# Moving two operations of a weight conversion from GpSimd to VectorE in a fused attention and MLP kernel

## The chip, the cores and the metric

The kernel runs on one core of a Trainium2 chip. The metric is the device time of one execution in microseconds (us). The core has TensorE (PE, matrix products; PEld is its weight load), VectorE (DVE), ScalarE (ACT), GpSimd (POOL), and queues that issue DMAs, here mostly that of SyncE (SP). The engines run side by side and meet at semaphores. Each engine works through its own instructions in a fixed order.

## The reference

Three layers, one behind the other, in float32. Shapes: batch 8, 8 heads, sequence 576, head width 64, 128 features; model width 512, inner width 1024.

```
# attention by features
proj = x @ w_phi;  proj -= max(|proj|) over features
phi(x) = concat(exp(proj), exp(-proj))
out = phi(q) @ (phi(k)^T v) / (phi(q) @ sum(phi(k)) + 1e-6)
# first MLP
xk = mu_k * x + (1 - mu_k) * x_prev     # x_prev: x shifted by one step
xr = mu_r * x + (1 - mu_r) * x_prev
k = relu(xk @ w_k);  v = (k * k) @ w_v;  r = sigmoid(xr @ w_r);  x = r * v
# second MLP
h = relu(x @ w_in);  c = conv over 3 steps of h;  out = (h * sigmoid(c)) @ w_out
```

The weights arrive as float64.

## The kernel before, in words

**Attention** works on 32 pairs of heads (`Pi`, four pairs to a batch). `block(Pi)` writes the work around one pair: at its head the transposes of pair Pi's centred q (`turn`, `turn_end`; tiles `pt`, `pr`), then the projection of k of pair Pi+2 (`front`; tiles `p`, `pk`, centred by VectorE as `mx` and `t`), of q of pair Pi+1 (`pq`), the sums over k and v (`sums4`, tile `pkv`), the quotients (`results`; tiles `pn`, `rd`, `xn`) and ScalarE's exponentials (`features`, tile `kp`). `column(Pi - 1)` and `column_end` transpose the finished pair's `xn` into `xT` (tile `px`). For pairs 1 to 3 that stands behind `front`; from `MS` = 4 on it stands at the head of the block, ahead of `turn`, so pair 3's transpose opens block 4.

**First MLP.** `moe(u)` works on half a batch u: mixed inputs (`xf`, `mh`, `ml`), eight products with w_k (`psk`), ReLU into `kf`, its square (VectorE, line 460), its high part `kh` (ScalarE) and low part `kl` (VectorE), four products with w_r (`psr`) and four with w_v (`psv`). Each float32 product is three matmuls of high and low parts (`mm3`, lines 149 to 151). From block 4 on `feed` puts 6, 6, 7, 9 and then 10 steps of it behind each block. TensorE runs in the order in which the program is written; the other engines' order is laid out by the framework's scheduler, which plans with modelled times, except where `behind` holds an instruction behind the one written before it on the same engine.

**The weights' conversion.** w_k, w_r and w_v are converted from float64 in 20 parts of 128 x 512 (`step`): a DMA into `raw` (two buffers), then a tick later ScalarE takes the absolute value of the high word into `h` (two buffers) and GpSimd clamps it, a tick later VectorE does a shift and two combining operations, a tick later ScalarE writes the high part (`wkh`, `wrh`, `wvh`) and GpSimd subtracts it to give the low part (`wkl`, ...). Each `tick` moves every part under way by one stage and starts the next part. So tick t brings the shift of part t-3 (counted from 0), and `ready` is t-3. Ticks stand twice in each of blocks 0 to 6 and, by `WAT`, nine more times behind blocks 4 to 6: 23 in all, as many as 20 parts need. `want(n)` adds ticks where a product needs parts that are not written yet. The tick that starts part i+2 waits on the SP queue for part i's `raw` buffer, which the second combining operation frees. w_in and w_out are converted later, by lines 120 to 134, in smaller parts (`hc`), still with GpSimd.

**Second MLP** runs after all that, from about 850 us, on the same engines.

Of the kernel before, what the change touches and what calls it, by code (L numbers as in the profile page):

```python
# [12 lines left out]
ALU = mybir.AluOpType  # L13
# [15 lines left out]
MS, SLOW, SR = 4, 8, {4: 6, 5: 6, 6: 7, 7: 9}  # L29

WAT = {4: (4, 10), 5: (3, 7, 11), 6: (3, 5, 7, 9)}
DS0 = 10
HS = S // 2
V1 = D + 1

# [6 lines left out]
def fused_kernel(ctx: ExitStack, tc: tile.TileContext, qk, va, wphi, ones2, mu, wk, wv, wr, win, wout, cw, out):  # L42
# [25 lines left out]
    V, A, G = Noted(nc.vector), Noted(nc.scalar), Noted(nc.gpsimd)  # L68
# [7 lines left out]
    def f(x):  # L76
        return x.bitcast(F32)
# [78 lines left out]
    with ExitStack() as p1:  # L156
# [10 lines left out]
        def step(src, hs, ls, o):  # L167
            o_ = slice(o, o + 512)
            raw = pool.tile([P, 512, 2], U32, tag="raw", bufs=2, name="raw")
            SY.dma_start(raw, src[:, o_])  # L170
            yield
            h = pool.tile([P, 512], F32, tag="h", bufs=2, name="h")
            high, low, hu = raw[:, :, 1], raw[:, :, 0], h.bitcast(U32)
            A.behind("activation", h, f(high), AF.Abs, scale=2.0 ** -16)
            G.behind("tensor_scalar", h, h, 2.0 ** -31, 122879.9921875 * 2.0 ** -16, ALU.max, ALU.min)
            yield
            V.behind("tensor_scalar", hu, hu, 3, None, ALU.logical_shift_left)
            V.scalar_tensor_tensor(hu, low, 29, hu, ALU.logical_shift_right, ALU.bitwise_or)
            V.scalar_tensor_tensor(hu, high, 0x7FFFFFFF, hu, ALU.bitwise_or, ALU.bitwise_and)
            yield  # L180
            A.behind("copy", hs[:, o_], h)
            G.behind("tensor_tensor", ls[:, o_], h, f(hs[:, o_]), ALU.subtract)
            ready[0] += 1

        under, ready = [], [0]

        def tick():
            for x in list(under):
                if next(x, 1) == 1:
                    under.remove(x)  # L190
            if wsteps:
                x = wsteps.pop(0)
                next(x)
                under.append(x)

        wsteps = [step(wk, wkh, wkl, o) for o in range(0, 4096, 512)]
        for h in range(2):
            for w in ((wr, wrh, wrl), (wv, wvh, wvl)):
                n = w[1].shape[1] // 2
# [13 lines left out]
        def load(Pi):  # L213

            b, p = divmod(Pi, NP)
            raw = pool.tile([P, W], F32, tag="x", bufs=3, name="rqk")
            if Pi == 0:
                for c in (slice(KC0, W), slice(0, KC0)):
                    SY.dma_start(raw[:, c], qk[b, p, :, c])
            else:  # L220
                (SY if Pi < 5 else G).dma_start(raw, qk[b, p])
            xk[Pi] = raw
# [86 lines left out]
        def column_end(xn, xt, px):  # L309
            T.transpose(px[:, :P], xn[:, 4], ident)  # L310

            def copies():
                for h in range(2):
                    r = slice(64 * h, 64 * h + 64)
                    A.copy(xt[r, 513:577], px[r, r])
            return copies
# [46 lines left out]
        def block(Pi):  # L363

            nq, nk = Pi + 1 < B * NP, Pi + 2 < B * NP
            if 0 <= Pi < B * NP - 3:
                load(Pi + 3)
            if Pi >= 0:
                if Pi >= MS:
                    x = column(Pi - 1)  # L370
                qf, t1 = turn(Pi)
                pr = psa.tile([P, 512], F32, tag="at", name="pr")
                if Pi >= MS:
                    copies = column_end(*x, pr)
                turn_end(qf, t1, pr)
                if Pi >= MS:
                    copies()
            if nk:
                tk = front(Pi + 2)
            if 0 <= Pi < 7:  # L380
                tick()
            if 1 <= Pi < MS:
                x = column(Pi - 1)
                column_end(*x, psm.tile([P, 512], F32, tag="mm", name="pr"))()
            if nq:
                ts[Pi + 1] += centre4(rows4(Pi + 1, 0, "pq"), "tq")
                del xk[Pi + 1]
                sums4(Pi + 1)
            if Pi >= 0:
                results(Pi, qf)  # L390
            if nk:
                features(Pi + 2, tk)
                if Pi + 2 > 1:
                    load_v(Pi + 2)
            if 0 <= Pi < 7:
                tick()

        def attention(Pi):
# [8 lines left out]
        def mix(u, j):  # L407

            b, hf = divmod(u, 2)
            o = hf * HS  # L410
            hi = main.tile([P, KC, HS], F32R, tag="mh", bufs=2, name=f"mh{j}")
            lo = main.tile([P, KC, HS], F32R, tag="ml", bufs=2, name=f"ml{j}")
            for c0 in range(0, KC, 2):
                xf = tmps.tile([P, 2, HS], F32, tag="tmp", name="xf")
                for c in range(c0, c0 + 2):
                    A.activation(xf[:, c - c0], xT[b, c][:, 1 + o:1 + o + HS], AF.Copy, scale=mu0[:, j, c:c + 1])
                    V.scalar_tensor_tensor(xf[:, c - c0], xT[b, c][:, o:o + HS], mu1[:, j, c:c + 1], xf[:, c - c0], ALU.mult, ALU.add)
                A.copy(hi[:, c0:c0 + 2], xf)
# [16 lines left out]

        def want(n):

            while ready[0] < n:
                tick()

        def moe(u):
            b, hf = divmod(u, 2)
            o = hf * HS
            for j in range(2):
                while not mix_next(u, j):
                    yield
            xh, xl = mixed.pop((u, 0))
            k2 = []
            for fp in range(FC // 2):
                kf = tmps.tile([P, 2, HS], F32, tag="tmp", name="kf")  # L450
                for j in range(2):
                    ps = psm.tile([P, 512], F32, tag="mm", name="psk")[:, :HS]
                    fc = 2 * fp + j
                    want(fc + 1)
                    for c in range(KC):
                        w = slice(fc * DM + c * P, fc * DM + c * P + P)
                        mm3(ps, wkh[:, w], wkl[:, w], xh[:, c], xl[:, c], c == 0, c == KC - 1)
                    A.activation(kf[:, j], ps, AF.Relu)
                    yield
                V.tensor_tensor(kf, kf, kf, ALU.mult)  # L460
                kh = main.tile([P, 2, HS], F32R, tag="kh", bufs=4, name="kh")
                kl = main.tile([P, 2, HS], F32R, tag="kl", bufs=4, name="kl")
                A.copy(kh, kf)
                V.tensor_tensor(kl, kf, f(kh), ALU.subtract)
                k2.append((kh, kl))
            rh, rl = mixed.pop((u, 1))
            for mp in range(2):
                sg = main.tile([P, 2, HS], F32, tag="sg", bufs=1, name="sg")
                for j in range(2):
                    ps = psm.tile([P, 512], F32, tag="mm", name="psr")[:, :HS]  # L470
                    mc = 2 * mp + j
                    want(9 + 6 * mp + j)
                    for c in range(KC):
                        w = slice(mc * DM + c * P, mc * DM + c * P + P)
                        mm3(ps, wrh[:, w], wrl[:, w], rh[:, c], rl[:, c], c == 0, c == KC - 1)
                    A.activation(sg[:, j], ps, AF.Tanh, scale=0.5)
                    yield
                mix_next(u + 1, mp)
                x2 = tmps.tile([P, 2, HS], F32, tag="tmp", name="x2")
                for j in range(2):  # L480
                    ps = psm.tile([P, 512], F32, tag="mm", name="psv")[:, :HS]
                    mc = 2 * mp + j
                    want(12 + 6 * mp + 2 * j)
                    for kc in range(FC):
                        w = slice(mc * DFF + kc * P, mc * DFF + kc * P + P)
                        kh, kl = k2[kc // 2]
                        mm3(ps, wvh[:, w], wvl[:, w], kh[:, kc % 2], kl[:, kc % 2], kc == 0, kc == FC - 1)
                    yield
                    V.scalar_tensor_tensor(x2[:, j], sg[:, j], 1.0, ps, ALU.add, ALU.mult)
                    yield  # L490
                SY.dma_start(x2s[b][:, 2 * mp:2 * mp + 2, o:o + HS], x2)
# [14 lines left out]
        def extras(Pi, n):  # L506
            if n in WAT.get(Pi, ()):
                tick()
            if Pi == 7 and n == 14:
                taps()  # L510
            if Pi >= DS0 and dsteps and n in (3, 11):
                dsteps[0] = dsteps[0][0](), dsteps[0][1]
            if Pi >= DS0 and dsteps and n in (4, 12):
                raw, step = dsteps.pop(0)
# [10 lines left out]
        with tc.manual_schedule(engines={mybir.EngineType.PE}):  # L525
# [6 lines left out]
            x = column(B * NP - 1)  # L532
# [160 lines left out]
```

## Time and profile before

| what | value |
|---|---|
| median of 3 runs | 1251.81 us (1251.13 to 1252.43) |
| the profiled execution | 1253.4 us |
| its span, first to last instruction | 1251.6 us |
| TensorE busy | 1210.5 us, 97% |
| VectorE busy | 771.0 us, 62% |
| ScalarE busy | 697.2 us, 56% |
| GpSimd busy | 133.9 us, 11% |
| mean granted clock of TensorE | 0.985 |

The profiled execution took 1253.4 us, 1.8 us more than the span that the trace covers and 1.6 us more than the median of the runs. Shares are over the whole span; the stretch that the change touches is its first eighth, and there they are others. A row of a stretch gives its start and end, its length, the busy time (and instructions) of PE, PEld, DVE, ACT and POOL, TensorE's mean granted clock as a share of 2.4 GHz, the busy share of the DMA engines and GB/s. A row of a group gives the total busy us, the mean ns of one, and the idle time ahead of them with what ended it; a row in order of time the start, the us, and in brackets the idle time before.

### The profile page before, as it was taken

The numbers are of one execution on the slowest core, as the hardware profiler recorded it, in microseconds if no ns is written. First come the engines' busy times: TensorE is split into PE (matmuls) and PEld (weight loads), VectorE is DVE, ScalarE is ACT, GpSimd is POOL, SyncE is SP. The second block draws the span as 40 slices with busy tenths as digits, with TensorE's granted clock in tenths as the row PEclk, the third lists the DMA queues.
The fourth block names the chain that finished last, engine by engine and source line by source line (L and its number), as shares of the span: only waits on it lengthen the run. The fifth ranks groups of instructions, "written<-read, shape, count | busy, mean of one in ns | idle before, by whom it ended". The sixth has DMA issues, their size and how long they took to land.

```text
span 1251.6 us, 29156 instructions
## 1 busy us (share of the span) xinstructions
PE 1210.5 (97%) x12000; PEld 1149.2 (92%) x12000; DVE 771.0 (62%) x1560; ACT 697.2 (56%) x1644; POOL 133.9 (11%) x219
## 2 busy tenths in 40 slices
PE   8798599999999999999999999999999999999998
PEld 7687599999999999999999999998888888888887
DVE  6989564767657657757655534425556655575555
ACT  6867274655656546646645534425555555565554
POOL 1445500111111111011000000000000000000000
PEclk9998699999999999999999999999999999999999
DMA  5534321223223223322220004050122011210210
GB/s 176 163 116 139 95 71 50 74 84 111 87 84 112 87 84 92 119 84 91 65 66 27 13 20 145 20 183 11 61 61 61 6 56 61 61 31 31 62 61 31
DMA packets 55956, 95.56 MB, mean 76 GB/s; under 512 B 10000, under 2 KB 38800, under 8 KB 55824
## 3 DMA queue, kind: packets, MB, share of 16 engines
q1 hardware_dynamic: 42544, 68.17, 16.9%
q0 software_dynamic: 3920, 15.93, 4.2%
q10 hardware_dynamic: 9360, 9.61, 2.8%
q8 instruction: 94, 1.54, 0.5%
q14 instruction: 38, 0.31, 0.1%
HBM read 66.42 MB, written 27.26 MB: 75 GB/s over the span
## 4 chain that ended last, share of the span: by engine, by line
PE 87%; DVE 6%; ACT 3%; issue 2%; DMA 2%; POOL 1%; SPq 0%; ACTq 0%; DVEq 0%; POOLq 0%
PE psh L149 5%; PE psh L151 5%; PE psh L150 5%; PE psv L149 5%; PE psv L150 5%; PE psv L151 5%; PE psk L150 5%; PE psk L151 5%; PE psk L149 5%; PE pkv L293 5%; PE pso L149 5%; PE pso L151 5%; PE pso L150 5%; PE pn L346 4%; PE psr L149 3%; PE psr L150 3%
## 5 line engine op out<-in xcount | busy, mean ns | idle before, releaser
L149 PE MATMUL psv<-kh,wvl 128*128 128x288 f32 x512 | 154.1, 301 | 11.6 <-POOL wvl L57 10.7
L57 DVE SCALAR_TENSOR_TENSOR ct<-h,cw,ct 128x460 f32<-128x460 f32 (+2 forms) x160 | 111.4, 697 | 85.2 <-ACT ct L57 84.1
L150 PE MATMUL psv<-kl,wvh 128*128 128x288 f32 x512 | 153.3, 300 | 2.1 <-DVE kl L57 2.1
L151 PE MATMUL psv<-kh,wvh 128*128 128x288 f32 x512 | 153.1, 299 | 0.0
L149 PE MATMUL psk<-mh,wkl 128*128 128x288 f32 x512 | 150.7, 294 | 1.3 <-ACT kf L57 1.3
L150 PE MATMUL psk<-ml,wkh 128*128 128x288 f32 x512 | 151.0, 295 | 0.0
L151 PE MATMUL psk<-mh,wkh 128*128 128x288 f32 x512 | 150.9, 295 | 0.0
L151 PE MATMUL psh<-xh,wih 128*128 128x462 f32 (+1 forms) x320 | 118.9, 372 | 0.0
L150 PE MATMUL psh<-xl,wih 128*128 128x462 f32 (+1 forms) x320 | 118.8, 372 | 0.0
L150 PE MATMUL pso<-gl,woh 128*128 128x460 f32 (+1 forms) x320 | 118.0, 371 | 0.0
L151 PE MATMUL pso<-gh,woh 128*128 128x460 f32 (+1 forms) x320 | 118.0, 371 | 0.0
L57 ACT ACTIVATE kf<-psk 128x288 f32<-128x288 f32 x128 | 52.2, 409 | 109.3 <-PE psk L151 108.5
L149 PEld LDWEIGHTS psv<-kh,wvl 128*128 128x128 f32 x512 | 97.9, 191 | 14.3 <-POOL wvl L57 12.3
L149 PE MATMUL psh<-xh,wil 128*128 128x462 f32 (+1 forms) x320 | 107.3, 372 | 0.0
L150 PEld LDWEIGHTS psv<-kl,wvh 128*128 128x128 f32 x512 | 98.2, 192 | 2.3 <-DVE kl L57 2.3
L151 PEld LDWEIGHTS psv<-kh,wvh 128*128 128x128 f32 x512 | 98.3, 192 | 0.0
L149 PEld LDWEIGHTS psk<-mh,wkl 128*128 128x128 f32 x512 | 96.3, 188 | 2.0 <-issue 1.3
L57 DVE TENSOR_TENSOR kf<-kf 128x576 f32<-128x576 f32 x64 | 48.7, 761 | 79.3 <-ACT kf L57 79.3
L150 PEld LDWEIGHTS psk<-ml,wkh 128*128 128x128 f32 x512 | 96.3, 188 | 0.0
L151 PEld LDWEIGHTS psk<-mh,wkh 128*128 128x128 f32 x512 | 96.2, 188 | 0.0
L57 DVE SCALAR_TENSOR_TENSOR x<-sg,psv 128x288 f32<-128x288 f32 x64 | 29.1, 454 | 108.1 <-PE psv L151 104.1
L57 ACT ACTIVATE h<-psh 128x462 f32<-128x462 f32 (+3 forms) x128 | 47.9, 410 | 75.5 <-PE psh L151 74.3
(96 smaller groups left out, 2866.5 us busy)
## 6 DMA issues: line engine op xcount, KB each, us to landing
rqk<-qk POOLq DMA_DIRECT2D x27, 576.0 KB, 4.7
va<-va SPq DMA_DIRECT2D x32, 325.0 KB, 4.2
x2s<-x SPq DMA_DIRECT2D x32, 288.0 KB, 2.2
raw<-wk SPq DMA_DIRECT2D x8, 512.0 KB, 3.5
raw<-wv SPq DMA_DIRECT2D x8, 512.0 KB, 3.5
raw<-win SPq DMA_DIRECT2D x16, 256.0 KB, 2.9
raw<-wout SPq DMA_DIRECT2D x16, 256.0 KB, 3.0
x2r<-x2s ACTq DMA_DIRECT2D x16, 231.0 KB, 2.7
```

Source lines behind the costliest of these rows:

```text
L57: x = op(*a, **k)
L149: T.matmul(ps, wl, xh, start=first, stop=False)
L150: T.matmul(ps, wh, xl, start=False, stop=False)
L151: T.matmul(ps, wh, xh, start=False, stop=last)
L293: T.matmul(o[r:r + 64], k_[:, r:r + 64], v_, start=(i == 0), stop=(i == len(prods) - 1))
L346: T.matmul(pn[b_][64 * r:64 * r + 64, j], qf[h_][:, c, o:o + 64], kv[:, c, h_], start=(j == 0 and c == 0), stop=(j == 4 - b_ and c == 1))
```

## The change

Five edits. VectorE takes the clamp and the low part's subtraction of the 20 parts from GpSimd; within a tick the high part's copy on ScalarE is now written first, then VectorE's operations of the next part, then the subtraction, then the absolute value, then the next load. Ticks also stand in block -1. `want` asks for two parts more than the product needs (`AHEAD`). ScalarE squares `kf` for the first batch (u = 0 and 1). Pair 3's `column` moves from the head of block 4 to the place behind `front`, with its last piece in a `psm` tile.

```diff
+AHEAD = 2
...
             A.behind("activation", h, f(high), AF.Abs, scale=2.0 ** -16)
-            G.behind("tensor_scalar", h, h, 2.0 ** -31, 122879.9921875 * 2.0 ** -16, ALU.max, ALU.min)
             yield
-            V.behind("tensor_scalar", hu, hu, 3, None, ALU.logical_shift_left)
+            V.behind("tensor_scalar", h, h, 2.0 ** -31, 122879.9921875 * 2.0 ** -16, ALU.max, ALU.min)
+            V.tensor_scalar(hu, hu, 3, None, ALU.logical_shift_left)
...
             A.behind("copy", hs[:, o_], h)
-            G.behind("tensor_tensor", ls[:, o_], h, f(hs[:, o_]), ALU.subtract)
+            yield
+            V.behind("tensor_tensor", ls[:, o_], h, f(hs[:, o_]), ALU.subtract)
             ready[0] += 1
...
-            for x in list(under):
-                if next(x, 1) == 1:
-                    under.remove(x)
+            for at in (3, 2, 4, 1):
+                for x in under:
+                    if x[1] == at:
+                        next(x[0], None)
+                        x[1] += 1
+            if under and under[0][1] == 5:
+                under.pop(0)
             if wsteps:
-                x = wsteps.pop(0)
-                next(x)
-                under.append(x)
+                under.append([wsteps.pop(0), 1])
+                next(under[-1][0])
...
-                if Pi >= MS:
+                if Pi > MS:
                     x = column(Pi - 1)
...
-            if 0 <= Pi < 7:
+            if -1 <= Pi < 7:
                 tick()
-            if 1 <= Pi < MS:
+            if 1 <= Pi <= MS:
                 x = column(Pi - 1)
...
-            while ready[0] < n:
+            while ready[0] < min(n + AHEAD, 20):
                 tick()
...
-                V.tensor_tensor(kf, kf, kf, ALU.mult)
+                if u < 2:
+                    A.square(kf, kf)
+                else:
+                    V.tensor_tensor(kf, kf, kf, ALU.mult)
```

## Rows read from the trace of the kernel before

**Rows 1.** The page's 40 slices: TensorE's granted clock in tenths.
```profile
PEclk9998699999999999999999999999999999999999
```
**Rows 2.** Stretches, blocks 0, 1, 4 to 7: length, then busy by engine.
```profile
15.20:23.80 8.60, 8.49 (x192) 7.92 (x190) 6.11 (x13) 8.01 (x23) 0.00 (x0) 1.00 0.45 137
23.80:33.80 10.00, 9.39 (x199) 8.54 (x195) 8.69 (x20) 8.37 (x24) 4.37 (x3) 1.00 0.25 82
...
62.35:85.11 22.76, 21.41 (x267) 20.48 (x268) 18.53 (x36) 15.24 (x37) 10.41 (x9) 0.87 0.41 129
85.11:112.40 27.29, 20.71 (x270) 19.15 (x269) 26.02 (x45) 19.11 (x46) 17.16 (x11) 0.94 0.37 112
112.40:155.65 43.25, 29.76 (x293) 27.36 (x292) 30.03 (x51) 18.43 (x43) 23.18 (x20) 0.74 0.38 115
155.65:177.65 22.00, 22.00 (x293) 21.64 (x293) 12.67 (x27) 12.48 (x33) 0.62 (x1) 0.97 0.18 58
```
**Rows 3.** The same view, all that follows block 6.
```profile
155.65:1251.60 1095.95, 1090.49 (x10272) 1038.88 (x10271) 643.86 (x1315) 599.30 (x1407) 62.04 (x155) 1.00 0.22 68
```
**Rows 4.** TensorE's waits, 0 to 156 us: total, times, longest.
```profile
PE psv L149 <- POOL wvl L57: 10.7, 5, 3.1
PE px L305 <- DVE xn L57: 5.2, 1, 5.2
```
**Rows 5.** The chain that ended last, 130 to 142 us.
```profile
130.18 3.60 DMA raw<-wv
...
133.87 0.69 ACT h L57
...
134.63 1.92 POOL h L57
...
136.72 1.26 issue
...
141.07 3.57 DMA raw<-wv
```
**Rows 6.** VectorE's instructions on `h`, 15.2 to 112.4 us: ns min/median/max, first and last start.
```profile
L57 DVE SCALAR_TENSOR_TENSOR h<-raw,h x26: 674/680/1664, 32.2 to 110.7; 128x512 uint32<-128x512 uint32 x26
L57 DVE TENSOR_SCALAR h<-h x13: 414/953/1500, 29.8 to 108.0; 128x512 uint32<-128x512 uint32 x13
```
**Rows 7.** VectorE's groups by form, 20 to 156 us.
```profile
L57 DVE SCALAR_TENSOR_TENSOR h<-raw,h 128x512 uint32<-128x512 uint32 x40 | 30.9, 772 | 0.5
L57 DVE TENSOR_SCALAR h<-h 128x512 uint32<-128x512 uint32 x20 | 19.2, 959 | 5.2 <-POOL h L57 5.2
...
L57 DVE TENSOR_TENSOR ml<-xf,mh 128x576 fp32r<-128x576 f32 x8 | 7.3, 914 | 0.0
...
L57 DVE TENSOR_TENSOR kf<-kf 128x576 f32<-128x576 f32 x4 | 3.2, 804 | 1.1 <-ACT kf L57 1.1
...
L57 DVE TENSOR_TENSOR kl<-kf,kh 128x576 fp32r<-128x576 f32 x4 | 3.0, 749 | 0.1
```
**Rows 8.** VectorE on `hc`, half as wide: ns min/median/max.
```profile
L57 DVE TENSOR_SCALAR hc<-hc x32: 282/286/290, 227.8 to 616.2; 128x256 uint32<-128x256 uint32 x32
L57 DVE TENSOR_TENSOR whl<-hc,whl x32: 415/418/420, 232.3 to 618.0; 128x256 fp32r<-128x256 f32 x32
```
**Rows 9.** VectorE in order of time.
```profile
62.47 0.42 DVE L57 TENSOR_SCALAR h<-h 128x512 uint32<-128x512 uint32 x1
...
66.57 0.29 DVE L57 TENSOR_REDUCE mx<-p 128x1 f32<-128x128 f32 x1 [2.24 <-PE p L236]
...
126.61 1.49 DVE L57 TENSOR_SCALAR h<-h 128x512 uint32<-128x512 uint32 x1 [0.53 <-POOL h L57]
```
**Rows 10.** GpSimd in order of time.
```profile
126.55 1.25 POOL L57 TENSOR_TENSOR wrh<-h,wrh 128x512 fp32r<-128x512 f32 x1
```
**Rows 11.** ScalarE's groups: `kh` (60 to 160 us) and table loads (whole span).
```profile
L57 ACT CAST kh<-kf 128x576 fp32r<-128x576 f32 x4 | 2.7, 682 | 2.2 <-DVE kf L57 2.2
...
L57 ACT ACT_TABLE_LOAD x2 | 2.6, 1283 | 1.2 <-PEq L684 1.2
```
**Rows 12.** ScalarE's waits, 20 to 156 us.
```profile
ACT h L57 <- DMA raw<-wv: 9.1, 4, 3.1
```

More of the change, by code (lines that the diff above doesn't have):

```diff
@@ L372, in block @@
                 pr = psa.tile([P, 512], F32, tag="at", name="pr")
-                if Pi >= MS:
+                if Pi > MS:
                     copies = column_end(*x, pr)
                 turn_end(qf, t1, pr)
-                if Pi >= MS:
+                if Pi > MS:
                     copies()
@@ L394, in block @@
                     load_v(Pi + 2)
-            if 0 <= Pi < 7:
+            if -1 <= Pi < 7:
                 tick()
```

## The prediction

> **What bounds the kernel now.** I read the 40 slices first. TensorE's granted clock is near full in all of them but the first few, and lowest in the fifth [rows 1]. Then the busy time by stretch, cut at each block's first transposes. From 155.65 us on TensorE is busy 1090.49 of 1095.95 us [rows 3]: nothing that VectorE, ScalarE or GpSimd do there is on the path, so the change can win or lose only ahead of that point. Block 6, 112.40 to 155.65 us, is where time lies open. It has 293 matmuls, as block 7 has, but takes 43.25 us where block 7 takes 22.00 with TensorE never idle; its clock is granted at 0.74, against 0.97 there [rows 2]. In block 5 VectorE is the full engine, 26.02 of 27.29 us. TensorE's waits say what is late: five times a low part that GpSimd wrote (10.7 us), and once, at the head of block 4, pair 3's `xn` (5.2 us) [rows 4]. The chain shows how block 6 goes round: a load (3.60 us), the absolute value, GpSimd's clamp (1.92), a gap of 1.26, VectorE's operations, which free the buffer, and the next load, 10.89 us after the first [rows 5].
>
> **The clamp and the subtraction.** VectorE gains 20 clamps and 20 subtractions. The clamp is a one-input operation of the shift's size; the shift takes 0.42 us when GpSimd does not run [rows 9]. Neighbouring VectorE rows overlap by some 0.08 us, so I count 0.34. A subtraction of 256 columns takes 0.418 us [rows 8] and one of 576 takes 0.749 [rows 7]; between them 512 come to 0.68, in the row 0.60. That is 20 x 0.94 = 18.8 us more. If the clamp, whose data are floats, went at the two-input pace, it would be 0.60 and the sum 5.2 us more; below 0.34 nothing points.
>
> Against that stands what GpSimd does to VectorE. The shift at 126.61 us took 1.49 us [rows 9], and GpSimd's subtraction had started 0.06 us before it, for 1.25 us [rows 10]: the shift ended 0.30 us after GpSimd did. In the mean a shift took 0.959 us, a combining operation 0.772, an `ml` 0.914 [rows 7]. Undisturbed they take 0.42 [rows 9], 0.68 (the median of the first 26 combining operations) [rows 6] and, as `kl` of the same size does, 0.75 [rows 7]. Without GpSimd's share VectorE gets back 20 x 0.54 = 10.8, 40 x 0.09 = 3.7 and 8 x 0.16 = 1.3: 15.8 us. The Trainium skill (SBUF — State Buffer, Terms) has a rule for this: VectorE and GpSimd share a pair of SBUF ports, taken for a whole instruction, and the loser "fully blocks". The trace agrees at 126.61 us. Read strictly, each of the 20 subtractions of GpSimd could hold VectorE for its whole 1.25 us, 25 us instead of 15.8, and the sum below would be 9 us lower; the mean of 0.772 us for the combining operations says that most did not meet one.
>
> **The squares.** Four of the first batch's squares lie ahead of 155 us. VectorE loses 3.2 us [rows 7], so its work changes by 18.8 - 15.8 - 3.2 = -0.2 us. ScalarE gains four operations as wide as `kh`, 0.68 us each [rows 11], 2.7 us, in blocks 4 and 5, where it is idle for 7.5 and 8.2 us [rows 2]. A square is not in the trace: from below, it cannot cost ScalarE less than nothing; from above, if it needed another function table, two loads of 1.28 us a time [rows 11] make 10.2 us more, still under that idle time. Without that cover it would delay `kh`, then `kl` and the first `psv`. I take nothing. The other four squares lie in blocks 7 and 8, where only TensorE counts [rows 3].
>
> **The ticks.** Two ticks in block -1 put every part two ticks earlier. In the old order 17 ticks, so 15 shifts, are written ahead of block 6, but only 13 start before 112.4 us [rows 6]: two lag, because each goes round through GpSimd. With GpSimd out of it I take a lag of one of 17, so three parts more are done ahead of block 6. A part costs VectorE 0.34 + 0.34 + 3 x 0.60 = 2.48 us, three 7.4. VectorE idles 2.5 us in block 0 and 1.3 in block 1 [rows 2]; I let half of these 3.8 hide some: +5.5 us, between 3.6 (all of it) and 7.4 (none).
>
> In block 6 four parts stay. The last subtraction is then written at the fourth tick of block 6 and its steps, ahead of the last two `psv` groups, which need parts 16 to 19. VectorE's work falls from 30.0 us by three parts to about 22.6. So the block lies between 22.00 us, what TensorE takes for the same 293 matmuls, and 30.0 us, what VectorE is busy now [rows 2]. I take the middle, 26: -17.25 us.
>
> **Asking two parts ahead.** I counted the ticks in the order of the program. With the new ones, `ready` is 9 at the first `psk`, 15 at the first `psr`, 16 at the first `psv`, 20 from the third `psr` on; nowhere less than two above what `want` asks for. So `AHEAD` adds no tick: nothing, and if I miscount, ticks that come anyway, a step earlier.
>
> **Pair 3's transposes.** They stand at the head of block 4, and TensorE waits 5.2 us there for `xn` [rows 4]. All else of block 4 is behind them, so VectorE, full until then, idles 2.24 us for `p` [rows 9]. Moved behind `front`, the wait has the pt, pr, p and pk matmuls ahead of it, and VectorE gets `p` at once: -2.2 us, between nothing (if VectorE fills the place with waiting work anyway) and -5.2. What is late next is VectorE's centring, not `xT`: `xn` comes when it did. Behind the moved transposes stand `pq` and `pkv`, which need VectorE's room as before.
>
> **The sum.** -17.25 - 2.2 + 5.5 - 0.2 = -14.15 us. On 1253.4 us, the profiled execution (span 1251.6 and 1.8 around it), that is 1239.25; the median of the runs is 1.6 us under that execution: 1237.7, say 1238. Its bounds: with 22.0, 5.2 and 3.6 it comes to 1229; with 30.0, nothing and 7.4 to 1246.
>
> **The rivals.** *The wait passes to the load* (faster by less). The load of part i+2 still waits for part i's buffer, and ScalarE waits for the load, 9.1 us in four waits of the `wv` parts [rows 12]. If parts in block 6 keep going round one by one, a round of 10.89 us loses the clamp on GpSimd (1.92) and the gap (1.26) and gains 0.34: 8.05 us. Three rounds save 8.5, the last subtraction some 0.7, so block 6 takes 34: -9.2 - 2.2 + 5.5 - 0.2 = -6.1, 1246. For it: the two buffers are unchanged. Against: two parts fewer are left there.
>
> *The ring of `h` holds ScalarE* (slower). The absolute value of part i+2 needs the buffer that part i's subtraction frees. That subtraction now stands on VectorE behind the four operations of part i+1: 2.0 + 0.6 us a tick, 5.2 a block. Exponentials and ReLUs queue behind that absolute value on ScalarE, TensorE waits for these. In block 1 ScalarE idles 1.6 us [rows 2]; blocks 2 and 3 I take alike. The hold beyond that is 3.6 us, 10.8 in three blocks; in block 6 the same hold keeps parts going one by one, so the tail is the former rival's: -6.1 + 10.8 = +4.7, 1256.5. It decides from 2.0 us a block on (6.1 / 3). For it: VectorE runs full there. Against: ScalarE's order is planned, and the plan can put exponentials ahead; and the hold matters only where ScalarE was ahead of VectorE.
>
> *Nothing comes of it*: the parts go to VectorE and the planned order puts them where they end no sooner than now, so the work (-0.2 us) is all that changes: 1251.6, no change.
>
> **How the numbers follow.** The forecast gets 0.66, the load 0.14, nothing 0.08, the ring 0.12. A measurement of this kernel tells about 0.2%, 2.5 us, from no change. So faster 0.80, same 0.08, slower 0.12. The range runs from the forecast's lower bound, 1229, to 1251: that takes in the load's 1246 with 5 us for a clamp at the two-input pace, and leaves out the ring and the tails.
>
> **What would show it.** Right: block 6 takes 22 to 30 us, TensorE's waits for a low part are gone or under 4 us, shifts all take about 0.42 us and clamps the same, about 16 shifts start ahead of block 6, the head of block 4 has no wait of 5 us, VectorE's busy time to the end of block 6 stays within some 3 us. Wrong: block 6 above 32 us with ScalarE waiting for loads (the load), blocks 1 to 3 longer by 2 us or more each with ScalarE waiting for VectorE's low part (the ring), or the instructions laid out by the scheduler in another order, so that a product's `kl` or `ml` comes late: that I cannot see from here.

## The result, and the profile after

The changed kernel takes 1242.05 us (median of 5 runs, 1239.62 to 1242.27), the kernel before 1251.85 in the same session (5 runs, 1251.13 to 1253.40): ratio 0.9914, 95% interval 0.9900 to 0.9929 (taken over all the runs; the quotient of the two medians is 0.9922). The profiled execution took 1242.27 us, its span is 1240.5 us, 11.1 less than before. It was faster, less than forecast.

The stretches of the kernel after, cut at the same first transposes: blocks 0 to 2, blocks 3 and 4, block 5, block 6, and the rest (start and end, length, busy time of PE, PEld, DVE, ACT and POOL, granted clock, DMA share, GB/s):

```profile
15.22:46.92 31.70, 28.06 (x582) 25.16 (x580) 29.82 (x70) 27.46 (x72) 1.08 (x2) 1.00 0.50 149
46.92:82.32 35.40, 31.94 (x463) 29.06 (x463) 33.84 (x79) 29.89 (x73) 1.06 (x2) 0.90 0.43 130
82.32:109.45 27.13, 21.56 (x270) 20.25 (x268) 25.00 (x52) 19.65 (x45) 0.53 (x1) 0.87 0.42 132
109.45:144.50 35.05, 26.36 (x294) 24.32 (x292) 29.79 (x63) 18.67 (x43) 1.49 (x6) 0.85 0.40 124
144.50:1240.50 1096.00, 1090.16 (x10274) 1038.34 (x10272) 640.90 (x1311) 602.05 (x1411) 61.87 (x155) 1.00 0.22 68
```

Blocks 0 to 2 took 30.16 us before (15.20 to 45.36), blocks 3 and 4 39.75 (to 85.11). Against these and [rows 2, 3] the five stretches differ by +1.54, -4.35, -0.16, -8.20 and +0.05 us: -11.1. Block 6 is the main gain, and it comes in two ways. TensorE's idle time there falls from 13.5 us (43.25 less 29.76) to 8.7, and its busy time for practically the same matmuls from 29.76 to 26.36, with the clock granted at 0.85 instead of 0.74. But the block is 9 us longer than forecast, and VectorE is busy there for 29.79 us: no less than before.

Block 4 began at 62.35 before and begins at 59.72 now, with no wait of 5 us at its head (TensorE in order of time; idle time before in brackets):

```profile
59.72 1.25 PE L330 MATMUL pt<-ident,t 128*128 128x128 f32 x8 [0.20 <-DVE t L58]
```

TensorE's waits in block 6 (total, times, longest), before and then after. They are still for low parts, which VectorE now writes, but take 7.3 us instead of 13.4:

```profile
PE psv L149 <- POOL wvl L57: 9.1, 4, 3.1
PE psr L149 <- POOL wrh L57: 4.3, 2, 2.4
```

```profile
PE psv L150 <- DVE wvl L58: 4.2, 3, 1.8
PE psr L150 <- DVE wrh L58: 3.1, 2, 2.7
PE pk L241 <- ACT xT L58: 1.4, 1, 1.4
```

In block 5, which is no shorter than before, TensorE now meets the conversion once as well, a wait that the profile puts down to a high part (before, low parts held it for 1.5 us there):

```profile
PE psv L150 <- ACT wvh L58: 4.8, 1, 4.8
```

VectorE's groups by form, 15 to 144.5 us (busy us, mean ns, idle time ahead), answer to [rows 7]:

```profile
L58 DVE SCALAR_TENSOR_TENSOR h<-raw,h 128x512 uint32<-128x512 uint32 x40 | 27.6, 689 | 0.6
L58 DVE TENSOR_SCALAR h<-h 128x512 uint32<-128x512 uint32 x20 | 8.5, 424 | 0.3
L58 DVE TENSOR_SCALAR h<-h 128x512 f32<-128x512 f32 x20 | 8.5, 423 | 3.2 <-ACT h L58 3.1
L58 DVE TENSOR_TENSOR ml<-xf,mh 128x576 fp32r<-128x576 f32 x8 | 6.0, 757 | 0.6 <-ACT mh L58 0.6
L58 DVE TENSOR_TENSOR wkl<-h,wkh 128x512 fp32r<-128x512 f32 x8 | 5.5, 689 | 0.0
L58 DVE TENSOR_TENSOR wvl<-h,wvh 128x512 fp32r<-128x512 f32 x8 | 5.5, 686 | 0.1
L58 DVE TENSOR_TENSOR wrh<-h,wrh 128x512 fp32r<-128x512 f32 x4 | 2.7, 686 | 0.0
```

The new clamps (423 ns) and subtractions (686 to 689) take what was forecast, and the shifts are down from 959 to 424 ns. What is not as forecast is how many parts were done by block 6. VectorE's clamps and shifts from the start of block 0 to that of block 6:

```profile
L58 DVE TENSOR_SCALAR h<-h x28: 416/424/428, 20.5 to 108.0; 128x512 f32<-128x512 f32 x14, 128x512 uint32<-128x512 uint32 x14
```

14 shifts, so six parts are left for block 6. Before it was 13 [rows 6]; the forecast had 16. Just ahead of block 6 the parts go one behind the other. VectorE and, below it, ScalarE in order of time, in the kernel after:

```profile
103.77 0.89 DVE L58 TENSOR_SCALAR h<-h 128x512 f32<-128x512 f32 x2
104.69 1.42 DVE L58 SCALAR_TENSOR_TENSOR h<-raw,h 128x512 uint32<-128x512 uint32 x2
106.03 0.69 DVE L58 TENSOR_TENSOR wvl<-h,wvh 128x512 fp32r<-128x512 f32 x1
107.50 0.89 DVE L58 TENSOR_SCALAR h<-h 128x512 f32<-128x512 f32 x2 [0.79 <-ACT h L58]
```

```profile
103.06 0.68 ACT L58 ACTIVATE h<-raw 128x512 f32<-128x512 f32 x1
106.14 0.62 ACT L58 CAST wvh<-h 128x512 fp32r<-128x512 f32 x1 [2.41 <-DVE h L58]
106.80 0.67 ACT L58 ACTIVATE h<-raw 128x512 f32<-128x512 f32 x1
```

VectorE's subtraction (`wvl`) of the previous part ends at 106.72 and frees one of the two buffers of `h`; ScalarE's absolute value of the next part starts at 106.80, and VectorE, with nothing else ready, idles 0.79 us for it. One round takes 3.73 us (103.77 to 107.50), of which VectorE works 2.95 (103.77 to 106.72). This is the ring of `h` that the prediction named as a rival. These rows alone do not prove it: ScalarE was itself copying a high part until 106.76, an instruction that stood ahead of the absolute value on its queue. The run with three buffers of `h`, below, tells more.

### The profile page after: what moved, and what is told of

Same layout as the page of the kernel before. It is cut to its first block, busy times and chain, and to the rows that moved or that the text cites. A ratio compares the mean times of both kernels' runs of the same rounds, so it can differ in the third digit from the quotient of the medians.

```text
span 1240.5 us, 29157 instructions
## 1 busy us (share of the span) xinstructions
PE 1207.8 (97%) x12000; PEld 1146.2 (92%) x12000; DVE 768.6 (62%) x1592; ACT 702.8 (57%) x1652; POOL 67.7 (5%) x179
## 3 DMA queue, kind: packets, MB, share of 16 engines
q8 instruction: 94, 1.54, 0.5%
## 4 chain that ended last, share of the span: by engine, by line
PE 89%; DVE 6%; ACT 3%; issue 1%; DMA 0%; SPq 0%; ACTq 0%; DVEq 0%
PE psv L150 5%; PE psh L150 5%; PE psh L152 5%; PE psh L151 5%; PE psk L151 5%; PE psv L151 5%; PE psk L152 5%; PE psv L152 5%; PE psk L150 5%; PE pkv L298 5%; PE pso L150 5%; PE pso L152 5%; PE pso L151 5%; PE pn L351 4%; PE psr L150 3%; PE psr L151 3%
## 5 line engine op out<-in xcount | busy, mean ns | idle before, releaser
L58 DVE TENSOR_TENSOR kf<-kf 128x576 f32<-128x576 f32 x56 | 42.5, 758 | 74.0 <-ACT kf L58 74.0
```

The costliest lines, as they stand in the source:

```text
L58: x = op(*a, **k)
```

## The experiments

All ratios are against the kernel before, with a 95% interval; the kernel after stands at 0.9914 [0.9900, 0.9929], and 0.001 is 1.25 us. The result and the experiments come from four sessions, so they are compared by these ratios and not by their medians. Where two intervals overlap, a difference of some 2 us between two experiments is not certain.

**The handover alone, and everything but the handover.** The first kernel takes `step` and `tick` of the kernel after into the kernel before; the second puts the old two back into the kernel after.

```diff
-            G.behind("tensor_scalar", h, h, ..., ALU.max, ALU.min)
...
+            V.behind("tensor_scalar", h, h, ..., ALU.max, ALU.min)
...
-            G.behind("tensor_tensor", ls[:, o_], h, f(hs[:, o_]), ALU.subtract)
+            yield
+            V.behind("tensor_tensor", ls[:, o_], h, f(hs[:, o_]), ALU.subtract)
...
+            for at in (3, 2, 4, 1):
```

> The kernel before with the handover alone (clamp and subtraction on VectorE, with the new order inside a tick); no tick in block -1, pair 3's transposes and the squares as before. If the handover carries the gain of block 6 (a part goes round faster without GpSimd), block 6 shortens by some 7 us, the head of block 4 keeps its wait of about 5 us for xn, and the time is 1244 to 1246. If the gain comes from the earlier ticks and the moved transposes, it is 1250 or more.

> The changed kernel with clamp, subtraction and the old order of a tick back on GpSimd; all else as changed. If the handover carries block 6, the block is again 40 us or more and the time is 1247 to 1249, the 4 us of the moved transposes being what is left. If ticks and transposes carry the gain, 1242 to 1244.

Measured: the handover alone 1249.79 us, ratio 0.9985 [0.9977, 0.9994]; all but the handover 1243.05 us, 0.9929 [0.9917, 0.9941]. So the handover is worth some 1.9 us either way (taken out, its interval overlaps that of the kernel after), and the theory that it carries the gain fell. In the first kernel block 6 falls to 36.90 us, but blocks 3 and 4 grow to 46.16 from 39.75, and pair 3's transposes, which still open block 4 there, wait 7.85 us instead of 5.2 [rows 4]. The stretches of blocks 3 and 4 and of block 6, handover alone:

```profile
44.54:90.70 46.16, 32.05 (x462) 29.86 (x463) 41.80 (x91) 31.34 (x77) 1.06 (x2) 0.89 0.38 120
...
117.46:154.36 36.90, 27.53 (x293) 25.68 (x292) 29.30 (x63) 18.64 (x43) 1.63 (x6) 0.84 0.38 120
```

TensorE in order of time, the same kernel:

```profile
64.09 0.47 PE L309 MATMUL px<-ident,xn 128*128 128x128 f32 x1 [7.85 <-DVE xn L57]
```

VectorE is busy 41.80 of the 46.16 us: the new work fills it, and `xn`, which goes through it as well, comes later. With everything but the handover 15 parts are ahead of block 6, which starts at 109.36 us, and block 6 still takes 35.57 us, because TensorE waits 9.75 us in one place (TensorE, then VectorE in order of time):

```profile
136.35 0.58 PE L150 MATMUL psv<-kh,wvl 128*128 128x288 f32 x1 [9.75 <-DVE x L58]
```

```profile
129.62 1.48 DVE L58 TENSOR_SCALAR h<-h 128x512 uint32<-128x512 uint32 x1 [2.69 <-POOL h L58]
...
133.63 1.49 DVE L58 TENSOR_SCALAR h<-h 128x512 uint32<-128x512 uint32 x1 [0.79 <-POOL h L58]
...
135.76 0.45 DVE L58 SCALAR_TENSOR_TENSOR x<-sg,psv 128x288 f32<-128x288 f32 x1
```

VectorE's `x` stands in its queue behind two shifts that wait for GpSimd's clamp. Fewer ticks at the head of block 6 should put `x` ahead of one of them:

```diff
-WAT = {4: (4, 10), 5: (3, 7, 11), 6: (3, 5, 7, 9)}
+WAT = {4: (4, 10), 5: (3, 7, 11), 6: (5, 7, 9)}
```

> The kernel with the handover undone, and block 6's later ticks at steps 5, 7, 9 instead of 3, 5, 7, 9, so that the first psv result x of block 6 is written ahead of the shifts that wait for GpSimd. TensorE waited 9.8 us for that x there. If its place behind these shifts is the reason, block 6 falls below 30 us and the time is 1234 to 1238, faster than the changed kernel without the handover. If the low parts are as late anyway, TensorE's wait turns into one for them: 1241 to 1244.

Measured: 1240.37 us, 0.9900 [0.9888, 0.9913]. The wait for `x` fell to 6.9 us and block 6 to 32.26: 3.6 us better than with that tick, but the wait is not gone, and the time lies between the two expected ranges. GpSimd's kernel is thus no worse than the kernel after, once the order suits it.

**The ticks.** Taken out of block -1 in the kernel after, and put there alone in the kernel before:

```diff
-            if -1 <= Pi < 7:
+            if 0 <= Pi < 7:
                 tick()
```

> The changed kernel without the two ticks in block -1. Changed, they brought one part more ahead of block 6 (14 shifts instead of 13) and blocks 0 to 2 became 1.5 us longer. If that is all of it, block 6 grows by one round of 3.7 us, blocks 0 to 2 give 1.5 back: about +2, 1244. If the ticks matter as the forecast had it (three parts), +5 or more, 1247. If VectorE, being full, decides alone, 1242.

> The kernel before with the two ticks in block -1 alone. Taking them from the changed kernel cost 0.4% (5 us). If that gain stands by itself, 1246 to 1247. If it needs a VectorE freed of squares and GpSimd, less than 2.5 us, 1250.

Measured: without them 1246.12 us, 0.9956 [0.9942, 0.9971]; they alone 1244.32 us, 0.9947 [0.9934, 0.9959], 6.6 of the 10.8 us. Block 6 of the kernel with the ticks alone takes 30.88 us, 4 less than in the kernel after, though GpSimd still clamps and subtracts and VectorE's shifts still take 987 ns in the middle. Its stretch of block 6, and its shifts ahead of it (ns min/median/max):

```profile
114.93:145.81 30.88, 25.79 (x293) 24.34 (x291) 23.97 (x45) 16.23 (x39) 17.69 (x16) 0.87 0.40 127
```

```profile
L57 DVE TENSOR_SCALAR h<-h x15: 409/987/1497, 21.1 to 110.7; 128x512 uint32<-128x512 uint32 x15
```

15 parts are ahead there, two more than before, for a start of block 6 that is 2.5 us later. The kernel without the two ticks, on the other hand, has 14 parts ahead of block 6, as many as the kernel after. What it loses lies earlier: its blocks 0 to 2 take 29.25 us instead of 31.70, its blocks 3 and 4 40.33 instead of 35.40 (VectorE busy for 38.24 instead of 33.84), so its block 6 starts 2.9 us later. The early ticks move work of VectorE out of blocks 3 and 4.

**Pair 3's transposes** back at the head of block 4:

```diff
-                if Pi > MS:
+                if Pi >= MS:
...
-            if 1 <= Pi <= MS:
+            if 1 <= Pi < MS:
```

> The changed kernel with pair 3's transposes back at the head of block 4. If their wait is worth what blocks 3 and 4 lost in the changed kernel, +4.3 us, 1246.4, with a wait of about 5 us for xn at the head of block 4. If only VectorE's idle time of 2.2 us counts, as forecast, 1244.3.

Measured: 1243.84 us, 0.9933 [0.9919, 0.9946], so the move is worth some 2.4 us by the ratios, though the intervals overlap. The wait is back, 6.1 us, and blocks 3 and 4 take 3.5 us more; block 5 gives 5.6 us back, block 6 takes 2.8 more.

**The squares** back on VectorE:

```diff
-                if u < 2:
+                if u < 0:
                     A.square(kf, kf)
```

> The changed kernel with the first batch's squares back on VectorE. VectorE, full in blocks 4 and 5, gets 3.0 us more ahead of block 6: if it bounds these blocks, +2 to +3, 1244 to 1245. If ScalarE's 2.7 us were as dear, no change, 1242.

Measured: 1244.72 us, 0.9939 [0.9927, 0.9950]: 3.1 us, as much as VectorE's 3.2 us of work, and in the block where VectorE is full. Block 5 takes 29.21 us instead of 27.13, VectorE busy for 27.24 of them; block 6 takes 1.7 us more too:

```profile
82.36:111.57 29.21, 21.87 (x270) 20.53 (x268) 27.24 (x57) 19.45 (x44) 0.53 (x1) 0.88 0.41 121
```

**The ring of `h`**: three buffers instead of two. For room, w_phi is held once instead of twice; block 0 starts at 15.25 us, as in the kernel after, so that has no effect of its own that can be seen; it was not run by itself, but with the clamp alone, below, the same two edits together bring nothing.

```diff
-            h = pool.tile([P, 512], F32, tag="h", bufs=2, name="h")
+            h = pool.tile([P, 512], F32, tag="h", bufs=3, name="h")
```

> The changed kernel with three buffers of h instead of two (room for it from w_phi held once instead of in two column blocks, the same numbers). If the ring of h paces block 6 (the absolute value of part i+2 waits for part i's subtraction, which stands behind part i+1's four operations, 3.73 us a round), the six rounds there become some 0.8 us shorter each and the time is 1237 to 1239. If VectorE's occupancy alone paces it, 1242.

Measured: 1238.28 us, 0.9880 [0.9864, 0.9896]: 4.3 us faster than the kernel after, and faster than both kernels. 15 parts are ahead of block 6, which starts 1.9 us later and takes 4.9 us less. What ScalarE's absolute value waits for in block 6 changes from VectorE's subtraction (3.1 us, once, in the kernel after) to the load, and once to VectorE's `t` (2.3 us). Just ahead of block 6 two absolute values now run one behind the other (102.21 and 104.98 us), with no copy of a high part between them. The stretch of block 6, then ScalarE's wait in it, three buffers:

```profile
111.35:141.53 30.18, 25.75 (x293) 24.33 (x292) 24.85 (x57) 16.74 (x41) 1.72 (x6) 0.90 0.43 131
```

```profile
ACT h L58 <- DMA raw<-wv: 3.0, 2, 2.2
```

**The same ring, opened by order**: in a tick the subtraction, which frees `h`, ahead of the next part's clamp, shift and combining operations.

```diff
-            for at in (3, 2, 4, 1):
+            for at in (3, 4, 2, 1):
```

> The changed kernel with the subtraction ahead of the next part's operations inside a tick. The absolute value is let go 2.3 us earlier, at the price of VectorE waiting up to 0.7 us a part for the high part's copy. If the ring of h paces block 6: 1239 to 1241. If VectorE's occupancy paces the blocks ahead of it, its waits cost more: 1243 to 1246.

Measured: 1246.94 us, 0.9958 [0.9944, 0.9972], 5.5 us slower than the kernel after. VectorE now stands at the subtraction until ScalarE has written the high part (4.3 us in four waits for `wvh`, 1.2 for `wrh`, 1.1 for `wkh`), and all that is queued on VectorE stands with it. Four operations of another part in between are a cover; the ring costs less than they save.

**The clamp alone on VectorE**, the subtraction back on GpSimd (kernel after, with the order of `sub_first`), and the two combinations with three buffers of `h`:

```diff
             yield
-            V.behind("tensor_tensor", ls[:, o_], h, f(hs[:, o_]), ALU.subtract)
+            G.behind("tensor_tensor", ls[:, o_], h, f(hs[:, o_]), ALU.subtract)
```

> The changed kernel with the subtraction back on GpSimd, written right behind the high part's copy; the clamp stays on VectorE. VectorE loses 12 us of subtractions ahead of 145 us but meets GpSimd's 1.26 us in some of its one-input operations again (0.54 us a shift before); the ring of h no longer runs through VectorE's queue. If the ring is what the handover gave up: 1236 to 1239. If VectorE's meeting with GpSimd is dearer: 1242 or more.

> Clamp and subtraction on GpSimd, old order in a tick, three buffers of h, all else as in the changed kernel. With two buffers this was 1.9 us slower than the changed kernel. If the third buffer takes the wait for GpSimd's subtraction away as it took that for VectorE's (4.3 us), 1238 to 1240, and the handover is worth 2 us at most in either. If GpSimd's longer round then paces, 1242 to 1244.

> Clamp on VectorE, subtraction on GpSimd, three buffers of h. If the two effects add up, 1233 to 1236, faster than every kernel so far. If the third buffer leaves nothing for the move of the subtraction, as with the changed kernel and three buffers, 1238.

Measured: the clamp alone 1239.20 us, 0.9906 [0.9892, 0.9919], not to be told from the kernel after; all but the handover, with three buffers, 1240.07 us, 0.9908 [0.9894, 0.9923], 2.6 us better than with two, though the intervals overlap; the clamp alone with three buffers 1239.64 us, 0.9913 [0.9898, 0.9929]. The last was expected to be the fastest of all and is a miss: a third buffer adds nothing to the clamp alone. The clamp alone has the shortest block 6 but one, and pays ahead of it; its stretch of block 6, and its combining operations over the 20 parts, slower again beside GpSimd's subtractions (824 against 689 ns):

```profile
114.41:141.87 27.46, 23.30 (x293) 22.39 (x292) 26.04 (x49) 15.22 (x38) 8.83 (x12) 0.94 0.40 130
```

```profile
L58 DVE SCALAR_TENSOR_TENSOR h<-raw,h 128x512 uint32<-128x512 uint32 x40 | 33.0, 824 | 0.5
```

**All versions side by side**, from their profiled executions; parts counted as shifts that start ahead of block 6:

| version | parts ahead | block 6 starts | block 6 | all after it | span |
|---|---|---|---|---|---|
| before | 13 | 112.40 | 43.25 | 1095.95 | 1251.6 |
| handover alone | 14 | 117.46 | 36.90 | 1095.4 | 1249.8 |
| subtraction first | 14 | 110.93 | 37.41 | 1097.1 | 1245.4 |
| ticks back | 14 | 112.32 | 35.93 | 1096.4 | 1244.6 |
| squares back | 14 | 111.57 | 36.75 | 1095.5 | 1243.8 |
| transposes back | 14 | 107.85 | 37.86 | 1096.0 | 1241.7 |
| after | 14 | 109.45 | 35.05 | 1096.00 | 1240.5 |
| ticks alone | 15 | 114.93 | 30.88 | 1095.5 | 1241.3 |
| handover back | 15 | 109.36 | 35.57 | 1096.0 | 1240.9 |
| the same, a tick less | 15 | 111.24 | 32.26 | 1095.9 | 1239.4 |
| three `h` | 15 | 111.35 | 30.18 | 1096.1 | 1237.6 |
| handover back, three `h` | 16 | 112.03 | 31.43 | 1096.2 | 1239.7 |
| clamp alone | 16 | 114.41 | 27.46 | 1095.9 | 1237.8 |
| clamp alone, three `h` | 16 | 112.73 | 27.45 | 1095.9 | 1236.1 |

The span is the sum of the three columns ahead of it, and the last of these moves little (1095.4 to 1097.1 us). Block 6 follows the parts left: 43 us with seven, 35 to 38 with six, 30 to 36 with five, 27 to 31 with four; the long ones with 15 parts are the two in which `x` waits for VectorE (9.8 and 6.9 us). A part done early shortens block 6 by 4 to 6 us and delays its start by 1 to 2.5 (ticks alone against before: two parts, 12.4 and 2.5; three `h` against after: one part, 4.9 and 1.9; clamp alone against after: two, 7.6 and 5.0).

These counts end at each version's own start of block 6, and a later start lets more parts be counted. At one time on the clock, 109.4 us, they lie closer: 12 with the handover alone, 13 before and with ticks or squares back, 15 in the three versions with three `h` and in the two others with the handover back, 14 in the rest. What holds without a count is that block 6 ends 5.5 to 9.6 us after the shift of the last part has started, in every version but one (handover back: 11.3).

## Why the prediction was right or wrong

The direction, the range and the place were right: 1242 against 1238, inside the forecast's own 1229 to 1246, the gain in block 6 and at the head of block 4, nothing after.

**The step that failed** is "With GpSimd out of it I take a lag of one of 17, so three parts more are done ahead of block 6". The lag is three, 14 of 17. The premise was that parts lag because they go round through GpSimd. Taking them from GpSimd brings none forward. The handover alone counts 14 of 15, but its block 6 begins 5 us later; up to 112.4 us, where block 6 began before, it has started 13 shifts, as the kernel before had [rows 6]:

```profile
L57 DVE TENSOR_SCALAR h<-h x26: 417/420/428, 29.9 to 111.9; 128x512 f32<-128x512 f32 x13, 128x512 uint32<-128x512 uint32 x13
```

And with the early ticks it is 15 by 109.36 us with GpSimd, 14 by 109.45 without. So GpSimd is not what holds them. Two things do. VectorE has little room for more: from 15 us to block 6 it is busy 88.88 of 94.45 us in the kernel after, and the squares' 3.2 us show up whole in the time. And the ring of `h` takes parts one by one, 3.73 us a round; a third buffer brings one part more ahead. The sum had a part at 2.48 us of VectorE; in such a round its five operations take 2.95, since an operation that stands right behind the one whose result it needs doesn't overlap with it.

**Block 6** was forecast at -17.25 and came to -8.2 with its six parts in place of four. VectorE's work there does not fall to 22.6 us: six parts at five rows each cost 19.5 us (9.0 + 2.5 + 2.5 for combining operations, shifts and clamps, 5.5 for eight subtractions), seven at three rows took 18.9 before. The forecast's 26 for four parts left is close to what two of the three versions with 16 parts ahead show (27.5; the third, which waits 5.4 us for GpSimd's low parts, 31.4), so the number of parts was the main error. All three still leave the subtraction to GpSimd; no version with the whole handover got to 16, so what its block 6 would take with four parts is not shown.

**Three parts earlier**, +5.5: one part came, and blocks 0 to 2 grew by 1.54 us. The same step failed here, in the other direction. With block 6 the two make -6.7 instead of -11.75.

**Pair 3's transposes**, -2.2: blocks 3 and 4 lost 4.35 us in the trace, inside the bound of 5.2; putting the move back costs 2.4. The forecast is close by the second, as far as the intervals tell. The 4.35 is not the move's own: with the move but without the early ticks blocks 3 and 4 take 40.33 us, no less than before (39.75).

**VectorE's work**, 18.8 more and 15.8 back: the rows give 22.2 us for 20 clamps and 20 subtractions, and 19.0 if each of the 40 overlaps by 0.08, which is the least, since those with a dependent operation right behind them don't; and back 10.7 for the shifts, 3.3 for the combining operations, 1.3 for `ml`, 15.3. The Trainium skill's rule (SBUF — State Buffer, Terms), read strictly, could have given 25 us back by the prediction's estimate; the rows do not show that. VectorE's busy time from block 0 to the end of block 6 went from 117.8 us to 118.5 with the squares gone, within the 3 us that the forecast allowed, and to 121.1 with the squares back.

**The squares** on ScalarE take 0.688 us each, within 0.006 of `kh`, with no further table load, and in the kernel after nothing waits for them, as forecast. That they are worth 3.1 us was not said: the prediction had entered VectorE's share in its balance, where it cancelled. **Asking two parts ahead**: no run took it out by itself; the prediction's count in the order of the program holds, so it adds no tick and does nothing.

**The rivals.** The load is not what holds block 6 in the kernel after (ScalarE waits for none there); it is what is late next, once `h` has three buffers. The ring of `h` exists, where the rival put it, but not at its price: blocks 1 to 3, which were to become 10.8 us longer, take 35.3 us instead of 38.6. Of what would show the forecast right, three signs failed: 14 shifts ahead of block 6 (16 were asked), waits for a low part of 7.3 us in block 6 (under 4), and a block 6 of 35 us (22 to 30). The waits read ahead of it were incomplete: beside the 10.7 us for `wvl` [rows 4] TensorE waited 4.3 us for the low parts of w_r.

**Which edit does it** was not as the sum had it either. Taken out one at a time the edits cost 5.3 (ticks), 3.1 (squares), 2.4 (transposes) and 1.9 us (handover), 12.7 together beside the 10.8 that they bring; the two smallest are near what the intervals can tell from nothing. Of the edits that do anything, the one with the most lines is worth least. The handover gives VectorE 3.7 us more work than it takes away (19.0 less 15.3); what it wins in block 6 without the other edits (6.35 us) it pays in blocks 3 and 4 (6.4).

**Open.** Why a third `h` adds nothing to the clamp alone; the spread of 1237.9 to 1242.4 us of that kernel hides 2 us. Whether the ring of `h` or ScalarE's order sets the round of 3.73 us: the third buffer changes both, so they are not told apart. What else holds `x` for 6.9 us with a tick less. No version has combined more buffers of `raw` with three of `h`, so whether the load then sets the end was not tried.

## What to carry to other kernels

When a stage that feeds TensorE lags, ask first whether the engine that it shares is full or a link is slow: here an earlier start of the same work (two ticks) was worth about three times what the removal of GpSimd's links was (6.6 and 1.9 us by themselves, 5.3 and 1.9 taken out). VectorE had 3.8 us free in blocks 0 and 1 [rows 2] for the earlier start; that this is the reason was not tried by itself. Count the parts that can be done by the deadline from the shared engine's free time and the buffers' round, not from the order in which they are written, and compare versions at one time on the clock where the deadline itself moves. With two buffers in a ring, look at what stands on the freeing engine's queue ahead of the instruction that frees one: a third buffer was worth 4.3 us, while freeing earlier by order cost 5.5.

## What the runs showed of the hardware

The overlap of some 0.08 us between VectorE's rows is not there between an operation and the one right behind it that needs its result. In the kernel after the subtraction starts at 106.03 us, 0.08 before the combining operation of another part ends, but of the operations of one part that stand right behind each other, each starts some 0.03 us after the end of the last (103.77 and 0.89 us, then 104.69). The squares on ScalarE (eight, 0.686 us each in the mean) brought no further load of a function table: both kernels have two, of 1.283 us [rows 11]. And TensorE's granted clock rose in block 6 as its idle time there fell: 13.5 us idle and 0.74 before, 8.7 and 0.85 after, 4.2 and 0.94 with the clamp alone, so that practically the same matmuls took 29.76, 26.36 and 23.30 us. Over these three each microsecond of wait that went brought about 0.7 more by the clock; other versions lie off that line (4.4 us idle and 0.90 with three buffers), so it is no rule.
